# Bucketed attention, MoE and ELU layer on one core: key hash products ahead of their comparisons, filler products out, second pair's values and third pair's query loads at other tiles

## The chip, the cores and the metric

The kernel runs on 1 core of one Trainium2 chip. The metric is the device time of one execution in microseconds (us). The profile is one execution of the program, taken by the hardware profiler; its times count from the start of the span.

## What is computed

An attention in which a query sees only the keys of its own hash bucket, then a mixture of 8 experts (one per token), then a layer with an ELU. Cut to what matters here:

```python
q_bits = (np.einsum('bhsd,dk->bhsk', q, proj) > 0)      # 6 bits per query, 6 per key
k_bits = (np.einsum('bhsd,dk->bhsk', k, proj) > 0)
mask = q_bucket[:, :, :, None] == k_bucket[:, :, None, :]
scores = np.where(mask, scale * np.matmul(q, k.transpose(0, 1, 3, 2)), -1e9)
attn = softmax(scores)
out = np.matmul(attn, v)                                 # 2 batches, 8 heads, 768 tokens, 64 per head
...                                                      # experts, ELU layer
```

## The kernel before

**Numbers in two parts.** Every fp32 operand is split into a high part (rounded to the type the array multiplies) and the remainder, and products are made of high times high, remainder times high, and high times remainder.

**Pairs and tiles.** The 16 heads are worked in 8 pairs. A head has 768 queries, which are 6 tiles of 128, so a pair is 12 tiles, and there are 96 tiles (`n` from 0). The loop over `n` is software-pipelined and written out by hand; the schedule is manual, so every engine runs its instructions in the order in which the program issues them. Per tile it issues
- `stage_S(n)`: the scores of tile n on the TensorE (PE). Two halves of 384 keys (`j`), each of two products that accumulate: one with `qa`/`ka` (line 326, 128 rows) and one with `qb`/`kb` (line 327, 102 rows). `kb` and `qb` hold, beside 64 rows of the split operands, the rows made from the hash bits, so that a key in another bucket gets a huge negative score.
- `stage_M(n-1)`: the row maximum `nm` on the VectorE (DVE, line 345), then `sc` and `bi` on GpSimd (POOL, lines 346 and 347).
- `stage_E(n-1)`: the exponential on the ScalarE (ACT, line 354), which needs `sc` and `bi` and frees the score buffer. There are two score buffers (`ps_s`), so the scores of tile n wait for the exponential of tile n-2.
- `stage_T(n-3)`: six transposes on PE (line 374), their evacuation `pthi` on ACT (line 376) and the remainder `ptlo` on DVE (line 377).
- `stage_V`: products of the attention with the values on PE (line 390), from tile 6 on.

**Preparing a pair.** The next pair is prepared while the present one runs: `prep_T` transposes the queries and keys (line 211) and splits them, `prep_Z` makes the hash products (line 237), `prep_V` splits the values on POOL (lines 304 and 305: a copy and a subtraction for two of the six blocks of one head), and `restack` copies rows to where `stage_S` wants them, with DMAs issued by the SyncE (SP, line 278). `load_pair` issues the loads from memory, also on SP (lines 128 and 134). The list `v_at` names the tiles of a pair at which `prep_V` is queued; it runs at the start of the next tile, on POOL behind that tile's `sc` and `bi`.

**Before tile 0** the program runs the preparation of pair 0 by itself: 15 filler products (`keep_warm`, line 602), the transposes, the key hash products `first_Zk(j)` into the two halves of one PSUM tile `zk` (line 243), their comparison with zero on DVE, `first_Ze` (line 250), the query hash products (`prep_Zm`, line 237), and their comparison. At tile 1 a second batch of 8 filler products is issued (line 678).

Of the kernel before, what the change touches and what calls it, by code (L numbers as in the profile page):

```python
# [21 lines left out]
MROWS = 32 + NBITS  # L22
# [3 lines left out]
def kernel(  # L26
# [15 lines left out]
    nc = tc.nc  # L42
# [3 lines left out]
    NC = S // 128  # L46
# [3 lines left out]
    HC = HALF * 128  # L50
# [47 lines left out]
    def load_piece(pc):  # L98
        i = pc % NP
        we1, we2 = w1[pc // NP], w2[pc // NP]  # L100
        t = raw_p.tile([128, PW], F32, tag="w", name="wraw")
        if i < 4:
            n = F // 4
            src = we1[:, i * n:(i + 1) * n].rearrange("(c p) f -> p c f", p=128)
        else:
            src = we2[:, (i - 4) * 128:(i - 3) * 128].rearrange("(c p) f -> p c f", p=128)
        nc.sync.dma_start(t.rearrange("p (c f) -> p c f", c=src.shape[1]), src)
        wraw[pc] = t
# [12 lines left out]
    def load_pair(pr, what="qkv"):  # L121
        b, h0 = divmod(2 * pr, H)
        for src, nm in ((q, "q"), (k, "k"), (v, "v")):
            if nm not in what:
                continue
            if nm == "v":
                t = ap2.tile([128, 2, NC * D], F32, tag="raw_v", name="raw_v")
                nc.sync.dma_start(t, src[b, h0:h0 + 2].rearrange("h (p c) d -> p h (c d)", c=NC))
            else:
                t = ap2.tile([128, NC, 2 * D], F32, tag="raw_" + nm, name="raw_" + nm, bufs=2 if nm == "q" else 1)  # L130
                step = HALF if (pr, nm) == (0, "q") else NC
                for c0 in range(0, NC, step):
                    for hh in range(2):
                        nc.sync.dma_start(
                            t[:, c0:c0 + step, hh * D:(hh + 1) * D],
                            src[b, h0 + hh].rearrange("(p c) d -> p c d", c=NC)[:, c0:c0 + step],
                        )
            raw[pr, nm] = t
# [19 lines left out]
    opnd = {}  # L158
# [30 lines left out]
    bd = {nm: (bdh[:, i], bdl[:, i]) for i, nm in enumerate("qk")}  # L189
# [49 lines left out]
            )  # L239

    def first_Zk(j):
        for i, (w, m) in enumerate(((bd["k"][0], khi), (bd["k"][0], klo), (bd["k"][1], khi))):
            nc.tensor.matmul(zk[:, j, 0:HC], w, m[:, j * HC:(j + 1) * HC], start=(i == 0), stop=(i == 2))

    def first_Ze(j, nm, c0=0, c1=HC):
        sl = slice(j * HC + c0, j * HC + c1)
        z = zk[:, j, 0:HC] if nm == "k" else zps[0, j][:, c0:c1]
        p0 = 0 if nm == "q" else 64
        ps = slice(p0, p0 + MROWS)
        nc.vector.tensor_scalar(  # L250
            opnd[0, nm + "b"][64:64 + MROWS, sl], z[ps], thr[ps, 0:1], amp[ps, 0:1], ALU.is_gt, ALU.mult
        )
# [61 lines left out]
    def tile_of(n):  # L314
        m, i = divmod(n, HALF)
        hd, hf = part_of(m)
        return hd, HALF * hf + i

    def stage_S(n):
        hd, c = tile_of(n)  # L320
        st = hd % 4
        ps = ps_s.tile([128, 2, 512], F32, tag="s", name="s")
        for j in range(2):
            sl = slice(j * HC, (j + 1) * HC)
            cb = slice(c * 128, (c + 1) * 128)
            nc.tensor.matmul(ps[:, j, 0:HC], opnd[st, "qa"][:, cb], opnd[st, "ka"][:, sl], start=True, stop=False)  # L326
            nc.tensor.matmul(  # L327
                ps[:, j, 0:HC], opnd[st, "qb"][0:64 + MROWS, cb], opnd[st, "kb"][0:64 + MROWS, sl],
                start=False, stop=True,
            )  # L330
        sps[n] = ps

# [64 lines left out]
    def stage_A(n):  # L397
        while add and add[0][0] <= n:
            _, t, w, u = add.pop(0)
            nc.gpsimd.tensor_tensor(t, w, u, ALU.add)  # L400
# [190 lines left out]
    def prep(pr, i):  # L591
        return prep_T(pr, "qqkk"[i], i % 2) if i < 4 else prep_Z(pr, i - 4)

    def both(fs):
        for f in fs:
            f()
# [19 lines left out]
    restack(0, "k", (1,))  # L616
    for j in range(2):
        first_Zk(j)
        first_Ze(j, "k")
    for nm in "qk":  # L620
        prep_Zm(0, 0, nm)
# [36 lines left out]
    v_at = (3, 5, 6, 8, 9, 11)  # L658
    todo = {}

    def at(n, f, *a):
        todo.setdefault(n, []).append((f, a))
# [12 lines left out]

            at(n0 + 8 * hf, start)
    at(1, second_half)
    at(1, keep_warm, 8)
    at(1, lambda: early.append(lambda: first_Ze(1, "q")))
    for j in range(2):  # L680
        at(2 + j, prep_Ze, 0, j)
# [75 lines left out]
    for pc in range(E * NP):  # L757
        stream.append((pc,))
        j, i = divmod(pc - W2P, 7)
# [160 lines left out]
    for n in range(NQ + 3):  # L920
        pr, s = divmod(n, 2 * NC)
        nx = pr + 1
        if NQ - 24 <= n < NQ - 12 and n % 3 == 0:
            load_piece((n - NQ + 24) // 3)
        if 1 <= n < NQ + 1:
            stage_M(n - 1)
        stage_A(n)
        both(early)
        early = []
        if 3 <= n < NQ + 3:  # L930
            m, part = divmod(n - 5, HALF)
            stage_T(n - 3, (lambda: stage_G2(m)) if m >= 0 and part == 0 else None)
        m, part = divmod(n - 4, HALF)
        if 0 <= m < NM and part == 0:
            stage_G(m)
        if late:
            late[0]()
        if n < NQ:
            stage_S(n)
        m, part = divmod(n - 13, HALF)  # L940
        if 0 <= m < NM - 3 and part == 0:
            early.append(stage_R(m))
        if n == NQ:
            stage_R(NM - 3)()
        m, part = divmod(n - 6, HALF)
        if 0 <= m < NM:
            stage_V(m, part)
        if 1 <= n < NQ + 1:
            stage_E(n - 1)
        if 0 <= m < NM and part == HALF - 1:  # L950
            stage_O(m)
        if late:
            late[1]()
            late = []
        for f, a in todo.pop(n, ()):
            f(*a)
        if n == NQ:
            ops_s.close()
            m2a = ctx.enter_context(tc.tile_pool(name="m2a", bufs=1, side="right", reuse_waits="tile"))
            split_piece(0, nc.gpsimd, nc.gpsimd, rest0)  # L960
            xt0 = [raw_p.tile([128, KD * CAP], F32R, tag="w", name="xt0") for _ in range(2)]
        if nx < NPAIR:
            i = s - 3 if pr == 0 else s // 3 * 2 + s % 3 - 1 if s % 3 else -1
            if 0 <= i < 6:
                late = prep(nx, i)
            if s in v_at:
                i = v_at.index(s)
                early.append(lambda a=(nx, i // 3, i % 3): prep_V(*a))
            if nx + 1 < NPAIR:
                if s == (6 if pr else 9):  # L970
                    load_pair(nx + 1, "qk")
                elif s == 11:
                    load_pair(nx + 1, "v")
    assert not todo
# [281 lines left out]
    for fb in range(W2A, FB2):  # L1256
        k = steps.index((0, fb))
# [8 lines left out]
    for k in range(NK):  # L1266
        ps = ff_L1(*steps[k])
# [129 lines left out]
```

## Time and profile before

| | us |
|---|---|
| three runs: median (lowest to highest) | 727.15 (724.84 to 727.83) |
| the profiled execution, device time | 725.06 |
| its span | 723.1 |
| PE busy | 706.4 (98%) |
| VectorE busy | 553.5 (77%) |
| ScalarE busy | 422.4 (58%) |
| GpSimd busy | 203.7 (28%) |
| PE granted clock, mean | 0.999 |

The span leaves out 1.96 us of the profiled execution's device time. The busy times are sums over stages with different limits; a matmul counts as busy to its modelled end, so neighbours overlap. The attention takes the span up to about 265 us, the experts follow, then the ELU layer.

### The profile page before, as it was taken

The numbers are of one execution on the slowest core, as the hardware profiler recorded it, in microseconds if no ns is written. First come the engines' busy times: TensorE is split into PE (matmuls) and PEld (weight loads), VectorE is DVE, ScalarE is ACT, GpSimd is POOL, SyncE is SP. The second block draws the span as 40 slices with busy tenths as digits, with TensorE's granted clock in tenths as the row PEclk, the third lists the DMA queues.
The fourth block names the chain that finished last, engine by engine and source line by source line (L and its number), as shares of the span: only waits on it lengthen the run. The fifth ranks groups of instructions, "written<-read, shape, count | busy, mean of one in ns | idle before, by whom it ended". The sixth has DMA issues, their size and how long they took to land.

```text
span 723.1 us, 12288 instructions
## 1 busy us (share of the span) xinstructions
PE 706.4 (98%) x4253; PEld 632.9 (88%) x4254; DVE 553.5 (77%) x1045; ACT 422.4 (58%) x843; POOL 203.7 (28%) x500
## 2 busy tenths in 40 slices
PE   8989999999999999999999999999999999999996
PEld 5779999999999988999999999788888888888885
DVE  5878988989898987788888887977688546944333
ACT  4777978879787875666666665454543224422221
POOL 6545454445545554011252241000000000002012
PEclk9999999999999999999999999999999999999999
DMA  7747577495774136987879886332222000001011
GB/s 165 183 104 178 153 183 185 124 216 136 167 208 108 76 103 208 304 241 231 263 238 248 196 234 198 93 109 77 72 88 87 31 1 1 1 0 59 0 59 61
DMA packets 108564, 97.39 MB, mean 135 GB/s; under 512 B 33448, under 2 KB 94696, under 8 KB 108496
## 3 DMA queue, kind: packets, MB, share of 16 engines
q1 hardware_dynamic: 106032, 90.15, 46.5%
q0 software_dynamic: 2304, 6.40, 2.4%
q8 instruction: 35, 0.57, 0.3%
q14 instruction: 33, 0.27, 0.1%
q10 hardware_dynamic: 160, 0.00, 0.0%
HBM read 64.15 MB, written 10.72 MB: 104 GB/s over the span
## 4 chain that ended last, share of the span: by engine, by line
PE 49%; issue 33%; DMA 7%; DVE 4%; ACT 4%; POOL 2%; SPq 1%; DVEq 0%; POOLq 0%; ACTq 0%
PE hps L1097 11%; PE yps L1110 8%; PE o L390 7%; PE t L374 6%; DMA out_dram<-part,tidt 4%; PE s L326 4%; PE s L327 3%; PE yps L1112 3%; PE zps L237 2%; PE sp L466 2%; ACT p L354 2%; DVE nm L345 1%; DVE ptlo L377 1%; PE prep L211 1%; PE xTp L1079 1%
## 5 line engine op out<-in xcount | busy, mean ns | idle before, releaser
L377 DVE TENSOR_TENSOR ptlo<-t,pthi 128x384 fp32r<-128x384 f32 x192 | 99.9, 548 | 29.0 <-ACT pthi L376 27.1
L354 ACT ACTIVATE p<-s,bi,sc 128x768 f32<-128x768 f32 x96 | 96.0, 1000 | 21.8 <-POOL bi L347 20.4
L376 ACT ACTIVATE pthi<-t 128x384 fp32r<-128x384 f32 x192 | 84.5, 497 | 26.4 <-PE t L374 25.7
L802 DVE TENSOR_TENSOR wl<-wraw,wh 128x1024 fp32r<-128x1024 f32 x63 | 77.0, 1225 | 22.3 <-ACT wh L799 19.4
L345 DVE TENSOR_REDUCE nm<-s 128x1 f32<-128x768 f32 x96 | 91.0, 948 | 1.2 <-PE s L327 1.2
L1211 ACT ACTIVATE ee<-gps 128x512 f32<-128x512 f32 x48 | 28.7, 597 | 97.9 <-PE gps L1201 97.9
L1249 POOL DMA_INDIRECT out_dram<-part,tidt x12 | 11.5, 959 | 263.6 <-DVE part L1246 262.2
L1110 PE MATMUL yps<-h,wh 128*128 128x448 f32 x256 | 84.4, 380 | 0.0
L374 PE MATMUL t<-ident,p 128*128 128x128 f32 x576 | 79.6, 273 | 0.7 <-DVE ptlo L377 0.6
L1201 PE MATMUL gps<-x2h,vl 128*128 128x512 f32 x192 | 75.9, 395 | 0.0
L1231 PE MATMUL a<-vh,gh 128*128 128x512 f32 x192 | 75.6, 394 | 0.0
L1231 PE MATMUL a<-vh,gl 128*128 128x512 f32 x192 | 75.4, 393 | 0.0
L326 PE MATMUL s<-ka,qa 128*128 128x384 f32 x192 | 73.6, 384 | 1.7 <-ACT p L354 1.1
L1201 PE MATMUL gps<-x2h,vh 128*128 128x512 f32 x192 | 75.3, 392 | 0.0
L1201 PE MATMUL gps<-x2l,vh 128*128 128x512 f32 x192 | 75.2, 392 | 0.0
L1231 PE MATMUL a<-vl,gh 128*128 128x512 f32 x192 | 74.9, 390 | 0.0
L374 PEld LDWEIGHTS t<-ident,p 128*128 128x128 f32 x576 | 67.4, 140 | 4.7 <-DVE ptlo L377 1.2
L1212 DVE TENSOR_SCALAR ee<-ee 128x512 f32<-128x512 f32 x48 | 20.4, 426 | 66.2 <-ACT ee L1211 66.2
L1214 ACT ACTIVATE gh<-ee 128x512 fp32r<-128x512 f32 x48 | 30.4, 633 | 69.2 <-DVE ee L1213 69.2
L390 PE MATMUL o<-pthi,vst 128*128 128x384 f32 x192 | 67.0, 349 | 0.8 <-ACT osb L411 0.6
L799 ACT ACTIVATE wh<-wraw 128x1024 fp32r<-128x1024 f32 x63 | 66.1, 1053 | 1.7 <-DMA wraw<-in_moe_w_dram 1.6
L327 PE MATMUL s<-kb,qb 102*128 102x384 f32 x192 | 65.3, 340 | 0.1
(212 smaller groups left out, 1774.6 us busy)
## 6 DMA issues: line engine op xcount, KB each, us to landing
wraw<-in_moe_w_dram SPq DMA_DIRECT2D x64, 512.0 KB
w<-in_moe_w_in_dram SPq DMA_DIRECT2D x16, 512.0 KB
w<-in_moe_w_out_dram SPq DMA_DIRECT2D x16, 512.0 KB
ka<-khi SPq DMA_DIRECT2D x30, 192.0 KB
xs_d<-zt SPq DMA_DIRECT2D x8, 528.0 KB
xs<-xs_d SPq DMA_DIRECT2D x8, 528.0 KB
raw_k<-in_k_dram SPq DMA_DIRECT2D x16, 192.0 KB
raw_v<-in_v_dram SPq DMA_DIRECT2D x8, 384.0 KB
```

The costliest lines, as they stand in the source:

```text
L326: nc.tensor.matmul(ps[:, j, 0:HC], opnd[st, "qa"][:, cb], opnd[st, "ka"][:, sl], start=True, stop=False)
L327: nc.tensor.matmul(ps[:, j, 0:HC], opnd[st, "qb"][0:64 + MROWS, cb], opnd[st, "kb"][0:64 + MROWS, sl], start=False, stop=True,)
L345: nc.vector.tensor_reduce(nm, sps[n][:, :, 0:HC], AX.XY, ALU.max, negate=True)
L354: nc.scalar.activation(p.rearrange("p (a b) -> p a b", a=2), sps.pop(n)[:, :, 0:HC], AF.Exp, bias=bi, scale=sc, accum_out=sums[hd][:, c:c ...
L374: nc.tensor.transpose(ps[:, a, :], p[:, kt * 128:(kt + 1) * 128], ident)
L376: nc.scalar.activation(ho, ps, AF.Copy)
L377: nc.vector.tensor_tensor(lo[:, HALF * g:HALF * (g + 1), i * 128:(i + 1) * 128], ps, ho, ALU.subtract)
L390: nc.tensor.matmul(ops[m], vst[hd][:, kt, :], t[:, kt, :], start=(kt == 0 and x == 0), stop=(kt == NC - 1 and x == 1))
L1097: nc.tensor.matmul(ps, w[:, dc, fs], x[:, dc], start=(i == 0), stop=(i == len(terms) - 1))
L1110: nc.tensor.matmul(ps, wh[:, f], h[:, :, f], start=(f == 0), stop=last)
L1201: nc.tensor.matmul(ps, w[:, dc], x[:, dc, th * TC:(th + 1) * TC], start=(dc == 0 and i == 0), stop=(dc == KD - 1 and i == 2),)
L1231: nc.tensor.matmul(ps, x[:, cs], w, start=(fb in first_fb and i == 0), stop=(fb in last_fb and i == 2))
```

## The change

1. `first_Zk` is called for both halves before the first comparison, where each half was followed by its comparison. In each half the product with the remainder of the weights comes second and the one with the remainder of the keys third; it was the other way round.
2. In tile 0 the two `qa`/`ka` products of the scores come ahead of the two `qb`/`kb` products; from tile 1 on they alternate as before.
3. The 8 filler products at tile 1 are gone.
4. During pair 0, the values of pair 1 are prepared at tiles 7 to 12, one piece each; it was tiles 4, 6, 7, 9, 10 and 12.
5. During pair 0, the query loads of pair 2 are issued at tile 6, its key loads stay at tile 9. Later pairs are as before.

```diff
     def first_Zk(j):
-        for i, (w, m) in enumerate(((bd["k"][0], khi), (bd["k"][0], klo), (bd["k"][1], khi))):
+        for i, (w, m) in enumerate(((bd["k"][0], khi), (bd["k"][1], khi), (bd["k"][0], klo))):
...
-        for j in range(2):
-            sl = slice(j * HC, (j + 1) * HC)
-            cb = slice(c * 128, (c + 1) * 128)
-            nc.tensor.matmul(ps[:, j, 0:HC], opnd[st, "qa"][:, cb], opnd[st, "ka"][:, sl], start=True, stop=False)
+        cb = slice(c * 128, (c + 1) * 128)
+        for j, x in ((0, "a"), (1, "a"), (0, "b"), (1, "b")) if n == 0 else ((0, "a"), (0, "b"), (1, "a"), (1, "b")):
+            n1 = 128 if x == "a" else 64 + MROWS
             nc.tensor.matmul(
-                ps[:, j, 0:HC], opnd[st, "qb"][0:64 + MROWS, cb], opnd[st, "kb"][0:64 + MROWS, sl],
-                start=False, stop=True,
+                ps[:, j, 0:HC], opnd[st, "q" + x][0:n1, cb], opnd[st, "k" + x][0:n1, j * HC:(j + 1) * HC],
+                start=(x == "a"), stop=(x == "b"),
             )
...
     for j in range(2):
         first_Zk(j)
+    for j in range(2):
         first_Ze(j, "k")
...
-    at(1, keep_warm, 8)
...
-            if s in v_at:
-                i = v_at.index(s)
+            v_s = v_at if pr else range(6, 2 * NC)
+            if s in v_s:
+                i = v_s.index(s)
                 early.append(lambda a=(nx, i // 3, i % 3): prep_V(*a))
             if nx + 1 < NPAIR:
-                if s == (6 if pr else 9):
-                    load_pair(nx + 1, "qk")
+                if s == 6:
+                    load_pair(nx + 1, "qk" if pr else "q")
+                elif s == 9 and pr == 0:
+                    load_pair(nx + 1, "k")
```

**PE, before tile 0.** The key hash products of the kernel before, with what each waits for (DVE_49 is the semaphore of the VectorE, Activation_49 that of the ScalarE):

```order
L243 MATMUL zk<-khi,bdh 128x384 [waits Activation_49]
L243 MATMUL zk<-klo,bdh 128x384 [waits DVE_49]
L243 MATMUL zk<-khi,bdl 128x384
L243 MATMUL zk<-khi,bdh 128x384 [waits DVE_49,Activation_49]
L243 MATMUL zk<-klo,bdh 128x384
L243 MATMUL zk<-khi,bdl 128x384
L237 MATMUL zps<-qhi,bdh 128x384 [waits Activation_49]
```

And of the changed kernel:

```order
L243 MATMUL zk<-khi,bdh 128x384 [waits Activation_49]
L243 MATMUL zk<-khi,bdl 128x384 [waits DVE_49]
L243 MATMUL zk<-klo,bdh 128x384 [waits DVE_49]
L243 MATMUL zk<-khi,bdh 128x384 [waits Activation_49]
L243 MATMUL zk<-khi,bdl 128x384
L243 MATMUL zk<-klo,bdh 128x384 [waits DVE_49]
L237 MATMUL zps<-qhi,bdh 128x384 [waits Activation_49]
L237 MATMUL zps<-qlo,bdh 128x384 [waits DVE_49]
```

The fourth product, the first of the second half, no longer waits for the VectorE; the waits that are left there are for `klo` and for `bdl`, the products' own operands.

**POOL, tiles 4 to 6.** Of the kernel before, from the `sc` of tile 3 on (`raw_v_255` holds the values of pair 0, `raw_v_293` those of pair 1; the `sc` after that are those of tiles 4 and 5):

```order
L346 TENSOR_SCALAR sc_366<-nm_364 128x1
L347 TENSOR_TENSOR bi_365<-sc_366,nm_364 128x1
L304 CAST vst_370<-raw_v_293 128x2x64
L305 TENSOR_TENSOR vst_370<-raw_v_293,vst_370 128x2x64
L429 TENSOR_SCALAR sm_385<-sums_264 128x3
L304 CAST vst_355<-raw_v_255 128x2x64
L305 TENSOR_TENSOR vst_355<-raw_v_255,vst_355 128x2x64
L346 TENSOR_SCALAR sc_404<-nm_402 128x1
```

And of the changed kernel (`raw_v_293` first comes behind the `sc` and `bi` of tile 6):

```order
L345 TENSOR_SCALAR sc_357<-nm_355 128x1
L346 TENSOR_TENSOR bi_356<-sc_357,nm_355 128x1
L428 TENSOR_SCALAR sm_373<-sums_264 128x3
L304 CAST vst_346<-raw_v_255 128x2x64
L305 TENSOR_TENSOR vst_346<-raw_v_255,vst_346 128x2x64
L345 TENSOR_SCALAR sc_392<-nm_390 128x1
```

The copy and subtraction of pair 1's values are gone from between the `bi` of tile 3 and the `sc` of tile 4.

**SP, tiles 6 to 11.** The queue around the query loads of pair 2 in the kernel before (`raw_q_632` are pair 2's queries, `raw_k_635` its keys; `kb3` and `qb3` are pair 1's operands):

```order
L278 DMA kb3_141<-z_574 6x768 x2
L278 DMA qb3_139<-z_574 12x768
L653 DMA rw_123<-in_moe_w_gate_dram 64x4x8
L653 DMA rw_123<-in_moe_w_output_gate_dram 64x4x8
L134 DMA raw_q_632<-in_q_dram 128x6x64 x2
L134 DMA raw_k_635<-in_k_dram 128x6x64 x2
L420 DMA o1_706<-o2_705 64x384
```

And in the changed kernel, around the same loads (`raw_q_473`):

```order
L278 DMA qa3_138<-qlo_350 64x768
L278 DMA qb3_139<-qhi_349 64x768
L134 DMA raw_q_473<-in_q_dram 128x6x64 x2
L278 DMA ka2_136<-khi_427 64x768 x2
L278 DMA kb2_137<-klo_428 64x768
```

The two query loads now stand ahead of pair 1's key restacking. On the way they pass 15 other transfers of the queue: six of that restacking, one of an output, six of the hash rows and two of the gate weights.

## Rows read from the trace of the kernel before

**Rows 1.** Who PE waited for, whole span: waiting line, releaser, total us, times, longest.
```profile
PE prep L211 <- DMA raw_q<-in_q_dram: 1.8, 1, 1.8
...
PE s L326 <- ACT p L354: 1.1, 2, 0.8
PE zk L243 <- ACT kb L612: 1.1, 1, 1.1
```
**Rows 2.** Windows: stretch, length, busy time (instructions) per engine, PEclk, DMA share, GB/s.
```profile
45.00:50.00 5.00, 3.18 (x22) 2.89 (x21) 2.45 (x6) 2.59 (x6) 1.12 (x6) 1.00 0.96 223
...
55.00:100.00 45.00, 44.99 (x303) 43.60 (x302) 38.55 (x73) 36.45 (x82) 21.85 (x70) 1.00 0.75 180
...
320.00:360.00 40.00, 40.00 (x316) 39.01 (x315) 33.80 (x57) 26.60 (x51) 7.13 (x4) 1.00 0.82 252
```
**Rows 3.** Timeline up to tile 1: start, duration, engine, line, what [idle before, releaser].
```profile
1.16 4.59 PE L602 MATMUL warm<-ones_b 128*128 128x384 bf16 x15 [1.16 <-DVE eb_b L81]
...
6.83 1.02 DVE L222 TENSOR_TENSOR klo<-prep,khi 128x384 fp32r<-128x384 f32 x2 [1.06 <-ACT khi L216]
...
7.77 0.55 DVE L220 SCALAR_TENSOR_TENSOR qlo<-prep,qhi 128x384 fp32r<-128x384 f32 x1
...
8.35 0.69 DVE L250 TENSOR_SCALAR kb<-zk,thr,amp 38x384 fp32r<-38x384 f32 x1
...
9.18 0.41 PE L243 MATMUL zk<-khi,bdh 128*128 128x384 f32 x1 [1.13 <-ACT kb L612]
...
11.06 0.85 DVE L250 TENSOR_SCALAR qb<-zps,thr,amp 38x128 fp32r<-38x128 f32 x2 [0.39 <-PE zps L237]
...
11.61 0.41 PE L327 MATMUL s<-kb,qb 102*128 102x384 f32 x1
...
12.41 0.96 DVE L345 TENSOR_REDUCE nm<-s 128x1 f32<-128x768 f32 x1 [0.50 <-PE s L327]
```
**Rows 4.** Timeline, tiles 1 and 2, around the filler products.
```profile
13.54 0.24 POOL L346 TENSOR_SCALAR sc<-nm 128x1 f32<-128x1 f32 x1 [2.25 <-DVE nm L345]
...
14.10 0.99 ACT L354 ACTIVATE p<-s,bi,sc 128x768 f32<-128x768 f32 x1 [2.22 <-POOL bi L347]
...
14.88 1.48 PE L602 MATMUL warm<-ones_b 128*128 128x384 bf16 x8
...
16.05 0.47 PE L326 MATMUL s<-ka,qa 128*128 128x384 f32 x1
```
**Rows 5.** Timeline, tiles 4 to 6, around the values of pair 1.
```profile
21.30 0.74 SPq L278 DMA_DIRECT2D qb<-z  x1
...
21.69 0.95 DVE L345 TENSOR_REDUCE nm<-s 128x1 f32<-128x768 f32 x1
...
22.49 0.29 POOL L304 CAST vst<-raw_v 128x128 fp32r<-128x128 f32 x1 [1.47 <-DMA raw_v<-in_v_dram]
...
24.51 0.22 POOL L346 TENSOR_SCALAR sc<-nm 128x1 f32<-128x1 f32 x1
...
25.04 0.99 ACT L354 ACTIVATE p<-s,bi,sc 128x768 f32<-128x768 f32 x1 [1.76 <-POOL bi L347]
...
26.18 0.44 PE L326 MATMUL s<-ka,qa 128*128 128x384 f32 x1 [0.81 <-ACT p L354]
```
**Rows 6.** Timeline, tiles 11 to 14, around the query loads of pair 2.
```profile
40.79 1.00 POOL L400 TENSOR_TENSOR osb<-o,o 64x384 f32<-64x384 f32 x1
...
42.96 1.01 ACT L354 ACTIVATE p<-s,bi,sc 128x768 f32<-128x768 f32 x1
43.06 1.78 SPq L134 DMA_DIRECT2D raw_q<-in_q_dram  x2
...
45.31 0.99 ACT L354 ACTIVATE p<-s,bi,sc 128x768 f32<-128x768 f32 x1 [0.38 <-POOL bi L347]
...
47.61 0.52 PE L211 MATMUL prep<-ident,raw_q 128*128 128x128 f32 x3 [1.82 <-DMA raw_q<-in_q_dram]
...
48.54 0.42 PE L326 MATMUL s<-ka,qa 128*128 128x384 f32 x1
```

## The prediction

> **What bounds the kernel now.** I read first who PE waited for, then the windows by stage, then the timeline of the first 50 us. The waits say that PE, the busiest engine, idles little, and mostly early: 1.8 us for the query loads of pair 2, 1.1 for a score buffer that an exponential frees, 1.1 in the key hash products [rows 1]. The windows say that behind them PE is full: 44.99 of 45 us from 55 on, all of 40 us in the experts, while from 45 to 50 it is busy for 3.18 of 5 [rows 2]. So the reader is to see a kernel bound by PE, with holes in its first 50 us; what closes a hole there should shift all that follows. The change touches nothing behind that point, so its worth is how much earlier tile 14 and what follows start. I follow that lead from stage to stage.
>
> **Key hash products first.** The fourth product starts at 9.18, after 1.13 us of idle time [rows 3]. The row puts this down to a ScalarE copy; I take the comparison on the VectorE instead, from 8.35 to 9.04, since it reads the same PSUM tile and the product's wait on the VectorE is the one that the new order drops. With all six products ahead, the last needs the second half of the key remainders, there at 6.83 + 1.02 = 7.85, and a product of this form shows about 0.41, so it is done by about 8.3. The first comparison waits for all six now, but the VectorE is busy with the query remainders until 7.77 + 0.55 = 8.32 anyhow, so it starts at 8.35 as before, and the second follows at 9.04 and ends at 9.73. Query hash products fit beneath it: one product is issued every 0.18 (8 fillers in 1.48 [rows 4]), so the five that want the query remainders go from about 8.4 to 9.2 and land by 9.5. Then the query comparison starts at 9.73 where it stood at 11.06: **1.33 us** earlier. In tile 0 the first `qb`/`kb` product follows that comparison (11.61 before [rows 3]); before, another `qa`/`ka` and `qb`/`kb` product came behind it, now one less, so 0.18 more. Lead of tile 0's maximum (12.41 before [rows 3]): **1.5**. Bounds: 1.0, if the comparison starts half a microsecond late behind the sixth product, and 1.6. The reordered products keep their number and widths, so by themselves they cost nothing.
>
> **Fillers out.** The exponential of tile 0 ends at 14.10 + 0.99 = 15.09, and frees the buffer of tile 2. The 8 fillers start at 14.88 and take 1.48, and tile 2 starts behind them at 16.05 [rows 4]. From the end of an exponential to the product that it frees is 0.15 (25.04 + 0.99 to 26.18 [rows 5]). So tile 2 could have started at 15.24, **0.8** earlier; the lead at tile 2 is 2.3. Bounds: 0, if rows that SP still has to place hold tile 3, and 0.8. What of loss there may be is the clock, a rival below.
>
> **Values of pair 1 later.** At tile 4 GpSimd waits 1.47 us for these values, until 22.49, and then works two pieces of values and a row sum; behind all that stands `sc` of tile 4, at 24.51. The maximum that it reads was done at 21.69 + 0.95 = 22.64 [rows 5], and `sc` of tile 0 starts 0.17 behind its maximum [rows 3, 4]: it is 1.7 late. The exponential follows with 1.76 of idle time, and then tile 6 on PE [rows 5]. Without the piece of pair 1 that hole goes, up to 1.76. I take **1.3**: next late is the VectorE, whose line of tile 5 (remainders, maximum) moves less than the exponential does. Bounds: 0, if tile 6 then waits for its hash rows (rival below), and 1.76. The lead at tile 7 is 3.6. The six pieces are moved, not removed: each costs GpSimd a copy and a subtraction, about 0.85 with its gaps (0.29 for the copy [rows 5]). They are not needed before tile 18, where the second pair's attention meets its values. At tile 11, where there was none, one now stands between the 1.00 us addition at 40.79 [rows 6] and the `sc` of that tile. The exponential of tile 11 begins at 42.96 behind other ScalarE work [rows 6], which covers about 0.55; cost **0.3**, bounds 0 and 0.85.
>
> **Queries of pair 2 at tile 6.** SP issues them at 43.06, and PE waits for them 1.82 us, until 47.61; tile 14 follows at 48.54. Without the wait it would start at 46.72, and its score buffer is free at 45.31 + 0.99 = 46.30 [rows 6], so all of **1.8** is had. Bounds: 1.2 (other transfers late) and 1.8. The two issues cost SP 1.78, now ahead of the 15 transfers that they pass. Cover: these serve tile 12 and later, and from tile 6 to tile 14 the kernel takes (48.54 - 26.18 - 1.82) / 8 = 2.6 us per tile [rows 5, 6], so over ten microseconds; without it the loss is up to 1.78 at tile 12. Key loads, the output transfer and the value loads behind them come 1.78 sooner.
>
> **Sum.** 1.5 + 0.8 + 1.3 - 0.3 + 1.8 = **5.1 us**. The profiled execution took 725.06; 725.06 - 5.1 = 720.0. That execution lies near the lowest of the three runs shown (median 727.15, mean 726.61), 1.55 below their mean, so for a set of runs I forecast 720.0 + 1.5 = **721.5 us**. All bounds at once on the low side give 1.0 + 0 + 0 - 0.85 + 1.2 = 1.4, which I don't expect together; on the high side 1.6 + 0.8 + 1.76 + 1.8 = 6.0.
>
> **Rivals.**
> *Transfers take the place.* The values of pair 1 land only at 22.49, and SP issues the last hash rows of tile 6 at 21.30 to 22.04 behind them [rows 5]. Tiles come earlier, the bytes don't shrink: if the backlog sets when these rows land, tile 6 waits for SP's transfers instead of GpSimd, the 1.3 is gone, and the query loads put in ahead cost half of their 1.78 at tile 12. Gain 5.1 - 1.3 - 0.9 = 2.9: 723.7 us. For it: the DMA share of 0.96 at 45 to 50 [rows 2] shows that bursts do fill the engines. Against: before, tile 6 was released by an exponential, not by a transfer, and the burst itself starts earlier with the query remainders.
>
> *The product waits for the ScalarE after all.* If the 1.13 in the key hash products ends with the copy, as the row has it [rows 3], the first term is lost but for 0.2: 722.8 us. Against: nothing in those operands comes from that copy.
>
> *The clock falls.* With the granted clock at 1.00 throughout, the 15 fillers at the start took 4.59 us, 0.31 each, the level of 1.2 GHz, and the 8 at tile 1 1.48, 0.185 each, that of 2.4 GHz [rows 3, 4]. If taking out the 8 lets PE fall back, each product costs 0.31 / 0.185 = 1.65 times as much. From tile 2 to tile 8 PE has some 15 us of products; at the low level that is 10 more: 721.5 + 10 = 731.5, slower. It decides from about 13 us of products at the low level on (0.65 times 13 is 8.7: the 5.1 and another 3.6). Against: from 45 to 50 PE sat idle for 1.82 in one piece, and the clock did not fall: the product behind, at 48.54, took 0.42 [rows 2, 6]; the new holes are no longer. The Trainium skill, "TensorE: Matmul & The Clock Gate", section "HAM oscillation — how this bites in real kernels", says that waits between bursts of products that last long enough put the array back to half rate, so that each burst starts cold; this speaks against taking fillers out. By that rule the time would be this rival's, by the rows it is the forecast's.
>
> **How the numbers follow.** About 0.5%, 3.6 us, is what a measurement of this kernel can tell from no change; faster by more is below 723.5. The forecast, all four holes mostly closed, gets 0.67; transfers 0.17, which lies on the edge, 0.05 of it below 723.5; the ScalarE rival 0.06, below it; the clock 0.04; 0.06 is left for holes that I don't see, half of it faster. So faster 0.67 + 0.05 + 0.06 + 0.03 = 0.81, which I lower to 0.79 as the terms hang together; slower 0.04; same 0.17. The range reaches from 718.5 (gain 6.0 with runs as low as the lowest, 724.84) to 724.7 (gain of 2.0 against the mean), which takes in the transfers and leaves out the clock.
>
> **What the profile would show.** Right: the fourth key hash product without a wait, tile 0's maximum near 10.9, tile 2 near 13.8, tile 6 near 22.5, no wait of PE for the query loads, tile 14 near 43.4, and windows from there on as full as before. Wrong: tile 6 or 12 released by a transfer; products of 0.31 apart after tile 2; or an early lead that a new wait at tiles 8 to 14 gives back.

## The result, and the profile after

The changed kernel takes 719.7 us (median of 4 runs, 719.5 to 719.86); the kernel before, run on the same chip beside it, 726.46 (4 runs, 724.84 to 727.83). The ratio is 0.9908, 95% interval 0.9885 to 0.993: faster by 0.9%. The profiled execution of the changed kernel took 719.73 with a span of 717.8, against 725.06 and 723.1 before: 5.3 us less, where the sum of the prediction was 5.1. The medians differ by 6.76.

The line numbers of the changed kernel are one or two lower, and both score products stand on line 326. Who PE waited for, whole span (waiting line, releaser, total us, times, longest):

```profile
PE s L326 <- ACT p L353: 1.1, 4, 0.4
...
PE zps L237 <- DVE qlo L220: 0.6, 1, 0.6
```

The two rows for the query loads and for the key hash products [rows 1] are gone. The total for the exponential is unchanged, but in four pieces of at most 0.4 where the longest was 0.8.

The windows, with the columns of [rows 2]:

```profile
45.00:50.00 5.00, 4.76 (x33) 4.43 (x32) 4.92 (x9) 4.54 (x11) 2.98 (x10) 1.00 0.60 141
55.00:100.00 45.00, 44.97 (x301) 43.63 (x300) 39.05 (x74) 35.55 (x81) 21.39 (x68) 1.00 0.68 165
320.00:360.00 40.00, 40.00 (x308) 38.82 (x307) 33.57 (x57) 26.73 (x51) 9.52 (x4) 1.00 0.78 237
```

The window from 45 to 50 is filled now (4.76 where 3.18 stood); the two behind it are as full as before. So the time came from the first 50 us, and the way to read it is the start of each tile's first score product:

| first score product, us | tile 1 | 2 | 6 | 11 | 13 | 14 | 16 | span |
|---|---|---|---|---|---|---|---|---|
| before | 12.21 | 16.05 | 26.18 | 39.55 | 44.12 | 48.54 | 53.36 | 723.1 |
| after | 10.74 | 13.76 | 22.17 | 35.52 | 40.70 | 43.11 | 48.06 | 717.8 |
| lead | 1.47 | 2.29 | 4.01 | 4.03 | 3.42 | 5.43 | 5.30 | 5.3 |

The lead grows at tiles 1, 2, 6 and 14, as the change was to make it, loses 0.6 between tiles 11 and 13, and then stays to the end of the program.

Timeline of the changed kernel up to tile 2 (start, duration, engine, line, what, idle before and releaser), to be laid beside [rows 3] and [rows 4]:

```profile
6.85 0.44 PE L243 MATMUL zk<-khi,bdh 128*128 128x384 f32 x1
...
7.72 0.34 PE L243 MATMUL zk<-khi,bdh 128*128 128x384 f32 x1
...
8.17 0.84 ACT L611 ACTIVATE kb<-klo 64x768 fp32r<-64x768 f32 x1
...
8.45 1.29 DVE L250 TENSOR_SCALAR kb<-zk,thr,amp 38x384 fp32r<-38x384 f32 x2
...
9.77 0.85 DVE L250 TENSOR_SCALAR qb<-zps,thr,amp 38x128 fp32r<-38x128 f32 x2
...
10.94 0.96 DVE L344 TENSOR_REDUCE nm<-s 128x1 f32<-128x768 f32 x1 [0.32 <-PE s L326]
...
12.63 0.99 ACT L353 ACTIVATE p<-s,bi,sc 128x768 f32<-128x768 f32 x1 [2.26 <-POOL bi L346]
...
13.76 0.44 PE L326 MATMUL s<-ka,qa 128*128 128x384 f32 x1 [0.20 <-ACT p L353]
```

The fourth key hash product starts at 7.72 without a wait, while the ScalarE copy of `kb` only starts at 8.17. Tile 2 now starts 0.14 behind the end of the exponential of tile 0 (12.63 + 0.99).

Tiles 4 to 6, beside [rows 5]:

```profile
20.43 0.23 POOL L345 TENSOR_SCALAR sc<-nm 128x1 f32<-128x1 f32 x1 [0.47 <-DVE nm L344]
...
20.97 0.99 ACT L353 ACTIVATE p<-s,bi,sc 128x768 f32<-128x768 f32 x1
...
22.17 0.42 PE L326 MATMUL s<-ka,qa 128*128 128x384 f32 x1
```

GpSimd waits for the maximum and no longer for a load, and neither the exponential nor tile 6 has idle time ahead of it. Tiles 10 to 16, beside [rows 6]:

```profile
32.71 0.72 SPq L419 DMA_DIRECT2D o<-o  x1
...
37.30 1.00 POOL L399 TENSOR_TENSOR osb<-o,o 64x384 f32<-64x384 f32 x1 [0.49 <-DMA o<-o]
...
39.56 0.99 ACT L353 ACTIVATE p<-s,bi,sc 128x768 f32<-128x768 f32 x1 [0.50 <-POOL bi L346]
...
40.70 0.44 PE L326 MATMUL s<-ka,qa 128*128 128x384 f32 x1 [0.38 <-ACT p L353]
...
42.21 0.49 PE L211 MATMUL prep<-ident,raw_q 128*128 128x128 f32 x3
...
43.11 0.42 PE L326 MATMUL s<-ka,qa 128*128 128x384 f32 x1
...
44.97 1.00 POOL L399 TENSOR_TENSOR osb<-o,o 64x384 f32<-64x384 f32 x1 [1.44 <-DMA o<-o]
```

The transposes of pair 2's queries don't wait. But GpSimd now waits 0.49 for an output transfer (`o<-o`) at 37.30, where it did not wait before, and by way of `sc` and the exponential of tile 11 this reaches tile 13. The wait of 1.44 at 44.97 is not new. In the kernel before it was more than twice as long:

```profile
50.27 1.00 POOL L400 TENSOR_TENSOR osb<-o,o 64x384 f32<-64x384 f32 x1 [3.22 <-DMA o<-o]
```

### The profile page after: what moved, and what is told of

Its sections match the earlier page's. It is cut to its first block, busy times and chain, and to the rows that moved or that the text cites. A ratio compares the mean times of both kernels' runs of the same rounds, so it can differ in the third digit from the quotient of the medians.

```text
span 717.8 us, 12271 instructions
## 1 busy us (share of the span) xinstructions
PE 705.1 (98%) x4245; PEld 632.2 (88%) x4246; DVE 553.1 (77%) x1045; ACT 422.2 (59%) x843; POOL 202.3 (28%) x500
## 4 chain that ended last, share of the span: by engine, by line
PE 51%; issue 33%; DMA 6%; DVE 4%; ACT 3%; POOL 1%; SPq 0%; DVEq 0%; ACTq 0%; POOLq 0%
PE hps L1099 11%; PE yps L1112 8%; PE s L326 7%; PE o L389 7%; PE t L373 7%; DMA out_dram<-part,tidt 5%; PE yps L1114 3%; PE zps L237 2%; PE sp L465 2%; ACT p L353 2%; PE prep L211 1%; DVE nm L344 1%; PE xTp L1081 1%; DVE ptlo L376 1%; PE warm L601 1%
```

## The experiments

Each is the changed kernel with one edit, unless it says otherwise. Since executions start unevenly (the last section), tiles are compared by their distance. `1-2` is the time from the first score product of tile 1 to that of tile 2, and so on; `16-end` is the rest of the span.

| us | 1-2 | 1-6 | 6-11 | 11-13 | 13-14 | 14-16 | 16-end | median (runs) |
|---|---|---|---|---|---|---|---|---|
| before | 3.84 | 13.97 | 13.37 | 4.57 | 4.42 | 4.82 | 669.7 | 726.57 (all 36) |
| after | 3.02 | 11.43 | 13.35 | 5.18 | 2.41 | 4.95 | 669.7 | 719.7 (4) |
| e11, the same again | 3.02 | 11.43 | 13.35 | 4.65 | 2.41 | 5.01 | 669.7 | 720.13 (5) |
| e1 fillers back | 3.84 | 12.25 | 13.38 | 4.63 | 2.41 | 4.72 | 671.3 | 719.87 (4) |
| e2 values back | 3.02 | 13.70 | 13.37 | 4.58 | 2.42 | 4.73 | 669.3 | 723.97 (10) |
| e5, the same again | 3.02 | 14.52 | 13.37 | 4.59 | 2.41 | 5.00 | 670.1 | 722.81 (1) |
| e6 values back, loaded early | 3.02 | 12.63 | 13.32 | 4.57 | 2.42 | 4.97 | 669.1 | 720.32 (4) |
| e3 queries back | 3.02 | 11.42 | 13.35 | 4.65 | 4.31 | 4.83 | 669.5 | 720.97 (5) |
| e7 queries at tile 4 | 3.02 | 11.43 | 13.63 | 4.66 | 2.42 | 4.86 | 670.0 | 719.01 (4) |
| e4 hash order back | 3.02 | 11.44 | 13.37 | 5.23 | 2.43 | 5.07 | 669.7 | 720.94 (6) |
| e8 values spread out | 3.01 | 11.41 | 13.34 | 4.16 | 2.40 | 5.48 | 670.9 | 719.51 (4) |
| e9 both of e7 and e8 | 3.03 | 11.45 | 13.35 | 4.15 | 2.40 | 5.23 | 669.3 | 719.05 (4) |
| e10 and keys behind the output | 3.02 | 11.45 | 13.34 | 4.16 | 2.40 | 4.72 | 669.2 | 718.96 (5) |

The nine runs of the changed kernel (after and e11) have a median of 719.73 and lie between 718.75 and 721.53. This spread sets what medians of four or five can tell: differences under about a microsecond are read from the distances alone.

### Fillers back (e1)

```diff
     at(1, second_half)
+    at(1, keep_warm, 8)
```

> The changed kernel with the 8 filler products put back at tile 1, nothing else. Chain theory (the fillers stand on PE between tile 1 and tile 2, and all behind them is shifted): in the changed kernel tile 2 starts at 13.76, as soon as its buffer is free; with the fillers, whose 8 products take 1.48, it should start 0.8 us later, near 14.6, and the span grow by 0.8, to 718.6. Rival (the early lead is swallowed by a later wait): tile 2 is 0.8 late, but tile 14 stands where it stood, 43.1, and the span grows by less than 0.2. Clock rival (fillers hold the clock up): the span shrinks, or the products behind are shorter; in the changed kernel they are 0.34 long with and without fillers.

Measured: 719.87 (719.62 to 721.06), ratio to the kernel before 0.9913 (0.988 to 0.9945). On PE around tile 2:

```profile
13.18 1.48 PE L601 MATMUL warm<-ones_b 128*128 128x384 bf16 x8
14.36 0.47 PE L326 MATMUL s<-ka,qa 128*128 128x384 f32 x1
```

Tile 2 is later by 0.82 (3.84 against 3.02), just the 0.8 that the prediction gave to the fillers, and tile 6 by as much. The median differs from that of the nine runs by only 0.14. Against the first profile of the changed kernel tile 14 is 0.3 later behind tile 1, and it looked as if tiles 11 to 13 swallow the rest; against the second (e11) it is 0.83. The swallowing was a difference between two executions of one kernel. So the 0.82 is shown in the early tiles; that the end gains as much is neither shown nor excluded.

### Values back at their old tiles (e2, e5)

```diff
-            v_s = v_at if pr else range(6, 2 * NC)
+            v_s = v_at
```

> The changed kernel with the second pair's values back at tiles 4, 6, 7, 9, 10 and 12. Chain theory: GpSimd waits again at tile 4, from the end of the bias of tile 3 at 18.75 until the values land, and the maximum of tile 4 is read behind it. In the changed kernel these loads are issued 1.47 us sooner than before (16.61 against 18.08) while the tiles are 2.3 sooner, so the wait should be longer than the 1.47 of before, about 2.2; the exponential of tile 4 then comes near 23.2 instead of 20.97, and with 0.4 won back at tile 11 the span grows by 1.5 to 2.0. Rival (transfers take the place, so that the values were not what held tile 6): tile 6 moves by less than 0.5 and the span grows by less than 0.5.

Measured: 723.97 (720.45 to 725.74, 10 runs), ratio to before 0.9966 (0.9946 to 0.9986): 4.2 us more than the nine runs of the changed kernel, and the widest spread of all versions of the changed kernel. The profiled execution is the fastest of the ten. To see a second one the same kernel ran again:

> The same kernel as in the run with the values back, once more, to see an execution nearer to its median of 723.97: its ten executions went from 720.45 to 725.74, and the one profiled was the lowest. Theory (the landing of the second pair's values varies from execution to execution, and GpSimd passes it on to all that follows): an execution at about 724 shows a wait of GpSimd for these values at tile 4 longer than the 2.03 us of the profiled one by about the difference in time, 3 to 4 us, and tile 6 later by the same. Rival (the spread comes from elsewhere): the wait at tile 4 is about 2 us again, whatever the time.

Measured: 722.81, span 720.9. Timeline of e2 at tiles 4 to 6:

```profile
20.48 0.29 POOL L304 CAST vst<-raw_v 128x128 fp32r<-128x128 f32 x1 [2.03 <-DMA raw_v<-in_v_dram]
...
21.67 0.18 DVE L436 RECIPROCAL ri<-sm 128x3 f32<-128x3 f32 x1 [1.12 <-POOL sm L428]
...
22.34 1.01 PE L373 MATMUL t<-ident,p 128*128 128x128 f32 x6 [1.20 <-DVE ptlo L376]
...
23.04 0.99 ACT L353 ACTIVATE p<-s,bi,sc 128x768 f32<-128x768 f32 x1 [2.32 <-POOL bi L346]
```

And of e5, the same four instructions:

```profile
21.75 0.29 POOL L304 CAST vst<-raw_v 128x128 fp32r<-128x128 f32 x1 [2.84 <-DMA raw_v<-in_v_dram]
...
22.94 0.18 DVE L436 RECIPROCAL ri<-sm 128x3 f32<-128x3 f32 x1 [1.94 <-POOL sm L428]
...
23.61 1.01 PE L373 MATMUL t<-ident,p 128*128 128x128 f32 x6 [2.02 <-DVE ptlo L376]
...
24.30 0.99 ACT L353 ACTIVATE p<-s,bi,sc 128x768 f32<-128x768 f32 x1 [3.14 <-POOL bi L346]
```

The wait of e2 and its exponential come about as expected, and tile 6 moves by 2.27, so the rival is out; the span grew by only 0.8, half of what was expected. Two things follow. First, the wait is not a size of the kernel but of the execution: 2.03 and 2.84 for one and the same kernel, and from tile 1 to tile 6 about the same amounts appear: 2.27 and 3.09 above the changed kernel. (The 1.47 of before [rows 5] belongs to other places of load and tiles, and is no third value of this.) Second, one late load holds two engines: behind GpSimd's copy stands the row sum `sm` (line 428), the VectorE's reciprocal waits for it, and behind that reciprocal stands the remainder that PE's transposes want. Of the 2.3 us between the two spans (718.6 and 720.9) the wait is only 0.82; 0.45 come from a later tile 1 (10.47 and 10.92), 0.27 between tiles 14 and 16, and 0.76 behind tile 16. So the landing shows as a part of the spread, not as all of it.

A second part goes with the granted clock, whose mean is on record for each run. It is 0.997 to 0.999 in all 46 runs of the changed kernel and of the versions without this wait (e6 too, where the pieces are at their old tiles). In e2 it is 0.992 to 0.996 in seven of ten runs, with a median of 724.25, and the other three have 721.41; in the kernel before it is 0.992 to 0.996 in 21 of the 32 runs beside the experiments, with a median of 726.89, and the other eleven have 725.33. Every kept trace is of a run at 0.997 or more, so none shows where that clock is lost, nor whether the late load brings it on. So of the 4.2 us the traces show 2.27 and 3.09, up to tile 6; what the rest is stays open.

### Values back, but loaded before tile 0 (e6)

```diff
+            v_s = v_at
...
     load_pair(0, "v")
+    load_pair(1, "v")
...
         load_pair(1, "k")
-        load_pair(1, "v")
```

> The changed kernel with the second pair's values back at tiles 4, 6, 7, 9, 10 and 12, but their load issued right behind that of the first pair's values, before tile 0, instead of at tile 1 behind the second pair's keys. Theory (the landing is the cost, not GpSimd's work at tile 4): no wait for values at tile 4, tile 6 within 0.5 us of the changed kernel (11.4 after tile 1), the time at 719.2 to 720.5, and the executions within 1.5 us of each other instead of 5.3. Rival (GpSimd's two pieces and the row sum between two maxima are the cost): tile 6 still 1 us late or more, time 721 and above, whatever the landing.

Measured: 720.32 (720.01 to 720.37), ratio 0.992 (0.9902 to 0.9937). GpSimd waits for no values; the transfer that gave way holds tile 3 instead:

```profile
17.30 0.42 PE L326 MATMUL s<-ka,qa 128*128 128x384 f32 x1 [1.28 <-DMA qa<-qlo]
```

Tile 6 is 1.20 late, where the theory allowed 0.5, but this wait of PE accounts for it, not GpSimd. The four runs lie within 0.36 us of each other. So with GpSimd's pieces at their old tiles, and the load alone moved, 3.7 of the 4.2 us come back. What the old places cost comes with the landing, not with GpSimd's work at tiles 4 and 6.

### Queries back at tile 9, and at tile 4 (e3, e7)

```diff
-                if s == 6:
-                    load_pair(nx + 1, "qk" if pr else "q")
-                elif s == 9 and pr == 0:
-                    load_pair(nx + 1, "k")
+                if s == (6 if pr else 9):
+                    load_pair(nx + 1, "qk")
```

> The changed kernel with the third pair's query loads back at tile 9, right ahead of its key loads. Chain theory: PE waits again before tile 14 for them; SP issues them at about 39.8, they land some 4.4 later, at 44.2, where PE wants them at 42.2: 2.0 us of wait, and the span grows by 1.8 to 2.0, to 719.7. Rival (an early lead only lengthens this wait, since the loads are bound by the DMA engines and not by the tiles): tile 14 stands near 48, as in the kernel before, and the span grows by 4 or more.

Measured: 720.97 (720.18 to 721.4), ratio 0.9926 (0.99 to 0.9951). The wait of before is back, at its old place and nearly its old size:

```profile
43.85 0.52 PE L211 MATMUL prep<-ident,raw_q 128*128 128x128 f32 x3 [1.71 <-DMA raw_q<-in_q_dram]
```

From tile 13 to tile 14 it costs 1.90 (4.31 against 2.41). GpSimd's wait for the output transfer behind tile 14 is back as well: 3.20, against 1.44 in the changed kernel and 3.22 before. Tile 13 itself came 0.53 sooner than in the first profile of the changed kernel, with no wait for `o<-o`, from which I took it that the early query loads delay the output transfer. To test that, the queries were issued two tiles earlier still, clear of it:

```diff
-                if s == 6:
+                if s == (6 if pr else 4):
```

> The changed kernel with the third pair's query loads at tile 4 instead of 6. In the changed kernel GpSimd waits 0.49 us at tile 11 for an output transfer, and tile 13 comes 2.73 after tile 12, where it is 2.19 with the loads at tile 9: the loads stand ahead of that transfer. Theory (they fill the DMA engines just when that transfer wants to go; two tiles sooner they fall into a gap of the engines): no wait for the output at tile 11, tile 13 about 0.5 sooner, span 717.3. Rival (any earlier load is late for somebody: the hash rows or restacked queries behind it on SP now come late): tile 6 or tile 12 waits for a transfer, and the time is that of the changed kernel or above it by up to 1 us.

Measured: 719.01 (718.9 to 719.94), ratio 0.9902 (0.9885 to 0.992); from tile 11 to tile 13 4.66, as the theory wanted, while the distance from tile 6 to 11 grew by 0.28. But e11 has 4.65 with the queries at tile 6, so this does not tell the theory from an execution in which the transfer happened to land in time.

### Key hash order back (e4)

The three edits of the hash products undone: the order of the products, the comparison behind each half, and the order of the four score products of tile 0.

```diff
-        for i, (w, m) in enumerate(((bd["k"][0], khi), (bd["k"][1], khi), (bd["k"][0], klo))):
+        for i, (w, m) in enumerate(((bd["k"][0], khi), (bd["k"][0], klo), (bd["k"][1], khi))):
...
         first_Zk(j)
-    for j in range(2):
         first_Ze(j, "k")
```

> The changed kernel with the key hash products and comparisons interleaved again, the order within a half as before, and tile 0 in the old order. Chain theory (the fourth product waits for the comparison on the VectorE, which reads the same PSUM tile): the product starts near 9.2 again instead of 7.72, the maximum of tile 0 near 12.4 instead of 10.94, and the span grows by 1.5, to 719.3. Rival (swallowed later): tile 0 is 1.5 late, tile 14 less than 0.5.

Measured: 720.94 (720.36 to 722.37), ratio 0.9932 (0.9909 to 0.9955).

```profile
7.96 0.83 ACT L611 ACTIVATE kb<-klo 64x768 fp32r<-64x768 f32 x1
...
8.95 0.41 PE L243 MATMUL zk<-khi,bdh 128*128 128x384 f32 x1 [1.12 <-DVE kb L250]
...
12.17 0.96 DVE L344 TENSOR_REDUCE nm<-s 128x1 f32<-128x768 f32 x1 [0.50 <-PE s L326]
```

The wait of 1.13 [rows 3] is back as 1.12, and this time the row names the VectorE. From the first key hash product to the maximum of tile 0 it takes 5.55 (12.17 - 6.62), against 4.09 in the changed kernel and 5.49 before: 1.46 by the distance, 1.2 by the medians. The two orders were undone together with the comparison; tile 0's alone was not run.

### One filler at the start instead of 15 (e12)

```diff
-    keep_warm(15)
+    keep_warm(1)
```

> The changed kernel with 1 filler product at the start instead of 15. It prices what the rival of the clock would have cost. If filler products matter to the clock at the start, the products before tile 0 stand 0.31 to 0.32 us apart (zk, zps) instead of 0.18, tile 0 and the tiles behind it come about 1 to 3 us later, and the fall would have shown in the changed kernel had the 8 fillers at tile 1 held the clock. If they don't matter at all, tile 0 starts no later than 9.6 and the products are as long as before.

Measured: 721.37, span 719.4 (one run), tile 1 at 12.20 against 10.74 and 10.40. PE before tile 0:

```profile
5.50 1.51 PE L211 MATMUL prep<-ident,raw_k 128*128 128x128 f32 x6 [3.83 <-DMA raw_k<-in_k_dram]
...
8.09 0.52 PE L243 MATMUL zk<-klo,bdh 128*128 128x384 f32 x1
8.41 0.52 PE L243 MATMUL zk<-khi,bdh 128*128 128x384 f32 x1
...
10.65 0.37 PE L237 MATMUL zps<-klo,bdh 128*128 128x384 f32 x1
10.86 0.34 PE L237 MATMUL zps<-khi,bdl 128*128 128x384 f32 x1
```

Behind 3.83 us of idle time, the products stand 0.32 apart, the level of 1.2 GHz, and from 10.86 on 0.17 to 0.18, that of 2.4 GHz; the latter is what the changed kernel shows before and behind tile 2. So a low level exists, costs this kernel 1.5 to 1.8 us by tile 1 (1.0 of it behind the first key hash product: 4.90 to tile 1, against 3.89), and would have been seen.

### Looking for a better version (e8, e9, e10), and the changed kernel again (e11)

```diff
-            v_s = v_at if pr else range(6, 2 * NC)
+            v_s = v_at if pr else (6, 7, 8)
...
+    for i, n in enumerate((12, 13, 15)):
+        at(n, prep_V, 1, 1, i)
```

> The changed kernel with the second pair's values at tiles 7, 8 and 9 (first head) and at the ends of tiles 12, 13 and 15 (second head, wanted from tile 24 on), so that no piece stands at tiles 10 and 11. Theory (what PE still waits there, 0.3 to 0.4 at tiles 11 and 13, comes from a maximum that GpSimd reads late behind a piece): the waits at tiles 11 to 13 shrink, tile 14 comes 0.3 to 0.7 sooner, span 717.1 to 717.5. Rival (ScalarE or VectorE bind there): tile 14 within 0.2 of the changed kernel's.

Measured: 719.51 (718.34 to 720.67), ratio 0.9904 (0.9884 to 0.9924); the span of the profile, 718.8, is above the expected 717.1 to 717.5. From tile 11 to tile 13 it takes 4.16, 0.49 less than in e11: so much do the pieces at tiles 10 to 12 cost (e9 and e10, below, have 4.15 and 4.16). Then 0.5 are lost from tile 14 to 16, with this row:

```profile
44.86 1.00 POOL L399 TENSOR_TENSOR osb<-o,o 64x384 f32<-64x384 f32 x1 [1.84 <-DMA o<-o]
```

e9 is e7 and e8 together; e10 has in addition the keys of pair 2 issued behind the output transfer, not ahead of it:

```diff
-                elif s == 9 and pr == 0:
-                    load_pair(nx + 1, "k")
                 elif s == 11:
-                    load_pair(nx + 1, "v")
+                    load_pair(nx + 1, "v" if pr else "kv")
```

> The changed kernel with both edits that have gained so far: the query loads of pair 2 at tile 4, and the values of pair 1 in pieces of the first head at tiles 7 to 9 and of the second at tiles 12, 13 and 15. If what is lost at tiles 11 to 13 has two separate causes (the output transfer behind the early query loads, and the piece of values on GpSimd), the gains add: tile 14 some 1.1 to 1.3 us earlier relative to tile 1 than in the changed kernel, and about 0.5 of that left at tile 16; a median near 719.0. If both edits close the same hole, tile 16 stands no earlier than with the values spread out alone (36.79 behind tile 1) and the median is 719.5.

Measured: 719.05 (718.22 to 719.88), ratio 0.9893 (0.9876 to 0.9909); tile 14 stands 31.35 behind tile 1, 1.02 sooner than in the first profile of the changed kernel and 0.49 sooner than in e11; tile 16 36.58. That is 0.2 better than e8, less than two executions of one kernel differ by; that the gains add is not shown.

> As the run before, and the key loads of pair 2 are issued behind the output transfer of tile 11 instead of ahead of it. Theory: GpSimd's wait of 1.3 to 1.8 us at tile 14 for that output transfer comes from the two key loads issued 2 us ahead of it, and it gives back half of what the spread values gain. Then the wait goes, tile 16 minus tile 1 is 36.3 or less (36.79 with the keys ahead), median near 718.5. Rival: the wait comes from the bytes in flight whatever their order; then the wait at tile 14 stays above 1 us and the median is the same within 0.3. If the keys land too late for their transposes (49.4 us in the changed kernel), a wait of PE for raw_k shows instead.

Measured: 718.96 (717.98 to 720.72), ratio 0.9896 (0.9877 to 0.9915). The wait is gone, which in e9 was (first row e9, second e10):

```profile
43.90 1.01 POOL L399 TENSOR_TENSOR osb<-o,o 64x384 f32<-64x384 f32 x1 [1.56 <-DMA o<-o]
...
43.17 1.01 POOL L399 TENSOR_TENSOR osb<-o,o 64x384 f32<-64x384 f32 x1
```

Tile 16 stands 36.07 behind tile 1, under the 36.3 that the theory wanted, where the rival wanted the wait to stay, and the keys are in time for their transposes. So it was the key loads ahead of the output transfer: counted from tile 1, SP now issues that transfer 1.86 us sooner (28.30 against 30.16 in e9), and the wait of 1.56 goes. Whether the loads held it by SP's time (their two issues took 1.77 in e9) or by their bytes is not told apart. The Trainium skill, "DMA: Bandwidth & Descriptors", section "Queues, rings and completion order", says that on each DMA engine descriptors are consumed in ring order; no run here shows the rings.

> The changed kernel itself, so that the two runs before have it beside them on the same chip. Expected 719.7 again, within 0.3.

Measured: 720.13 (718.75 to 721.53), ratio 0.9909 (0.9893 to 0.9926), 0.43 above 719.7 where 0.3 was allowed. Its profile has no wait for the transfer ahead of tile 13, and the same wait behind:

```profile
31.71 0.55 SPq L419 DMA_DIRECT2D o<-o  x1
...
36.42 1.00 POOL L399 TENSOR_TENSOR osb<-o,o 64x384 f32<-64x384 f32 x1
...
39.83 0.44 PE L326 MATMUL s<-ka,qa 128*128 128x384 f32 x1
...
44.16 1.00 POOL L399 TENSOR_TENSOR osb<-o,o 64x384 f32<-64x384 f32 x1 [1.47 <-DMA o<-o]
```

So e10 is the best by the distances (tile 16 behind tile 1: 36.07, against 37.32 and 36.85 in the two profiles of the changed kernel) and by the median on the same chip, 718.96 against 720.13; the intervals of the two ratios overlap, and 1.2 us on five runs each is not shown as a gain of the whole.

## Why the prediction was right, and where it was off

The forecast was faster, 721.5 with a range of 718.5 to 724.7; 719.7 lies in it. That the sum of 5.1 comes so near the 5.3 between the two profiles is in part luck: its terms came out at 1.40, 0.82, 1.72 and 2.01, together 6.0, of which one execution lost 0.6 at tiles 11 to 13; the second profile of the changed kernel (e11, span 716.9) lies 6.2 below the one of before. Two slips of the working carry no weight: 0.65 times 13 is 8.5 and not 8.7, and the lowest run less 6.0 is 718.8 and not 718.5. Step by step:

**Key hash products: 1.5 forecast, 1.40 in the profile.** From the first key hash product to the maximum of tile 0: 5.49 before, 4.09 after. Of this the order in tile 0 has 0.18, as worked out (from the query comparison to the maximum: 12.41 - 11.06 = 1.35 before, 10.94 - 9.77 = 1.17 after). The rival that the product waits for the ScalarE is refuted: it starts at 7.72, ahead of the copy, and e4 names the VectorE.

**Fillers: 0.8 forecast, 0.82 at tile 2** (3.84 to 3.02), and again 0.82 when they are put back.

**Values: 1.3 forecast, 1.72 in the profile.** This is the term that was mis-sized. The lead grew from 2.29 at tile 2 to 4.01 at tile 6. The text said "next late is the VectorE, whose line of tile 5 (remainders, maximum) moves less than the exponential does", and took 1.3 of 1.76 for it. But the VectorE was late by the same load, through `sm` and the reciprocal, in the kernel before as in e2 and e5:

```profile
23.68 0.18 DVE L437 RECIPROCAL ri<-sm 128x3 f32<-128x3 f32 x1 [0.57 <-POOL sm L429]
...
24.36 1.01 PE L374 MATMUL t<-ident,p 128*128 128x128 f32 x6 [0.64 <-DVE ptlo L377]
```

So both came free, and nearly the whole bound of 1.76 was the value. The medians of the runs show 4.2 for the old places (e2). That is more than any trace shows, and part of it goes with a lower granted clock.

**From the profiled execution to the median.** The 1.5 us were added because the profiled execution of before lay below the mean of its runs. By the result they should have been left out: 720.0 instead of 721.5, and 719.7 came. The nine runs of the changed kernel have a median of 719.73, the time of its first profile, and none of them has the lower granted clock that 21 of 32 runs of before have. The eleven others of before, at 0.997 or more, have a median of 725.33, 5.6 above these nine, near the 5.3 of the profiles. So the change took that part away with the wait; that the wait caused it is not shown.

**The tile where a piece was added: 0.3 forecast.** In the first profile 0.6 were lost from tile 11 to 13, in the second 0.08 (4.65 against 4.57). The piece itself is the small part; the 0.5 that the two executions differ by come with the wait for `o<-o` at 37.30. That all pieces at tiles 10 to 12 cost 0.49 was seen in e8. Part of that wait is the early query loads. SP issues the output transfer 5.26 and 5.47 us ahead of tile 11 where the query loads come behind it on the queue (e3 and before), and 2.81 to 4.77 ahead in the twelve profiles where they come first. The two with the wait are the latest, 2.81 (35.52 - 32.71) and 2.89 (e4), and the transfer lands 4.6 to 4.7 behind its issue; e11 has 3.47 (35.18 - 31.71) and no wait. So the loads take much of the slack, and half a microsecond elsewhere on SP's queue seems to decide the rest.

**Queries: 1.8 forecast, 2.01 from tile 13 to 14** (4.42 to 2.41, and 2.41 in e11 too); 1.90 when put back (e3), of which the medians show 1.2. The cover named for the 15 transfers held for PE, which waits for none of them; GpSimd's wait at 37.30 is the exception, in two profiles.

**The rivals.** *Transfers take the place* did not happen at tiles 6 and 12, where it was looked for; it did happen in small ahead of tile 13, with the 0.49 for the output transfer. The later wait of 1.44 is no loss: it is 1.78 shorter than before, as much as the prediction had that transfer come sooner. *The clock* did not fall in the changed kernel: behind the longest gap at tile 2 (0.63) the products still take 0.34, with starts 0.17 to 0.18 apart, the level of 2.4 GHz, and the mean granted clock of its nine runs is 0.997 to 0.999. The Trainium skill, "TensorE: Matmul & The Clock Gate", section "HAM oscillation — how this bites in real kernels", says that waits between bursts that last long enough put the array back to half rate; here no hole did, and putting the fillers back (e1) gained nothing. So the rule was no argument against taking these 8 out. At the very start, where PE comes from 3.83 us of idle time, taking fillers out does cost (e12), which agrees with it.

## What to carry to other kernels

When an in-order engine waits for a load, read everything queued behind the waiting instruction and every engine that waits for any of it: here a copy that nobody needed before tile 18 held the exponential by one path and the transposes by another. A wait for a transfer has the length of one execution. When the runs of a kernel lie above its profile, look at their granted clocks before the difference is added to a sum: here it went away with the change. And before a difference of half a microsecond between two kernels is explained, profile one of them twice.

## What was not expected of the hardware

Executions differ in three places, by as much as some of the edits. The first is the start: tile 1 of kernels with the same start begins between 10.40 (e11) and 11.32 (e10). The rows of e11, then of e10:

```profile
1.16 4.15 PE L601 MATMUL warm<-ones_b 128*128 128x384 bf16 x15 [1.16 <-DVE eb_b L81]
5.40 0.85 PE L211 MATMUL prep<-ident,raw_k 128*128 128x128 f32 x6
...
1.16 4.98 PE L601 MATMUL warm<-ones_b 128*128 128x384 bf16 x15 [1.16 <-DVE eb_b L81]
5.94 1.43 PE L211 MATMUL prep<-ident,raw_k 128*128 128x128 f32 x6
```

No wait for the key loads stands there. The 15 fillers themselves take 0.28 us each in one and 0.33 in the other, and the key transposes behind them 0.85 and 1.43, the latter near the 1.51 of e12. In e10 PE is still at the level of 1.2 GHz when the fillers end; in e11 it had left that level before. The second is the wait for `o<-o` ahead of tile 13, which is there or not. The third is the rest of the span behind tile 16, 669.1 to 671.3: in e1 and e8, the two longest, PE waits in the experts for GpSimd's scaling of the gathered rows, a wait that no other profile shows (the row of e1):

```profile
PE xTp L1082 <- POOL xs L824: 1.4, 1, 1.4
```

The granted clock does not tell the two levels of the start apart. In e12 the products before 10.65 stand 0.32 apart, and the window reads 1.00 all the same (its columns as above):

```profile
6.00:10.50 4.50, 4.50 (x18) 4.50 (x17) 2.57 (x5) 2.93 (x5) 2.74 (x6) 1.00 0.81 179
```

So the level is read from the distance of equal products, not from the column.
